# Chunked SSD attention and a GELU MLP on one core: the decay loads first, C scaled by GpSimd, a new order of the steps, and wide products in stage 1

## The chip, the cores and the metric

The kernel runs on one core of a Trainium2 chip. The time is device microseconds of one launch. A core has five engines that run side by side: TensorE (PE, with its weight loads PEld), VectorE (DVE), ScalarE (ACT), GpSimd (POOL) and SyncE (SP), which issues most of the DMAs.

## The reference

An attention over chunks (a state space model: 4 batches, 8 heads, 768 positions, head size 32, state size 16) gives 3072 rows of 256 columns, and a two-layer MLP with a tanh GELU follows.

```python
# per chunk of the sequence
cum = np.cumsum(log(clip(a)), axis=-1)
L = np.exp(cum[:, :, :, None] - cum[:, :, None, :]) * causal
M = einsum('bhin,bhjn->bhij', Cc, Bc) * L
y = einsum('bhij,bhjd->bhid', M, xc) + einsum('bhin,bhnd->bhid', Cc, state) * exp(cum)
state = exp(sum(la)) * state + sum over j of (B_j outer x_j) * exp(cum_last - cum_j)
# then, x = y as [3072, 256]
h = x @ w_in                       # 256 x 2048
out = gelu_tanh(h) @ w_out         # 2048 x 256
```

## The kernel before, in words

The sequence is cut into chunks of 128 positions, 6 for each of 4 batches, 24 in all. Two chunks make a pair `u` (0 to 11) of 256 tokens; pairs 0, 1 and 2 are batch 0.

The kernel is a list of named steps. A table, `ORDERED`, writes the order of all steps out by hand, and the engine that takes a step where there is a choice (`:A` ScalarE, `:D` VectorE, `:P` GpSimd, `:S` SyncE). Each engine runs its own instructions in that order. A word `~n` is a filler: matmuls of zeros, n times 128 columns, into the bank `yb`.

The front works for batch 0:

- `load_aq.0` to `load_aq.3` load the decays `a` of the first four chunks (four 16 KB loads into `aq_t`, on the queues of SyncE and ScalarE), `load_bc0.1` loads C and `load_bc0.0` loads B of these chunks (256 KB each into `bcf`), `load_x4` loads x, `load_a` the rest of the decays, `load_wi` and `load_wo` the four blocks each of w_in and w_out, 512 KB apiece.
- On VectorE, `clipq` (L328) clips the decays into `acq`, `Rq` (L331) scans them, `tpq` (L342) transposes, `recip0` (L348) takes the reciprocal `pt`. `mulb` (L416) scales B by the decays, `mulc.0` and `mulc.1` (L409) scale C by the reciprocals into `cz`, which `c_cz` has filled with zeros. `peq`, `c_sel` (the tiles `sel` and `selp`) and the small product `ppq` give `pendq`, the decay of each chunk.
- `tw.i` (L425) transposes the scaled C and B on TensorE, `ew.w.i` evicts the transposes (`ce`, `bh`). `x4` casts x.
- `XX.u` and `XD.u` (L563, L573) unpack x and form the state terms of pairs 0 and 1, `xn` evicts x. `c_bmask` builds a mask `bmask` on GpSimd, `c_par` reduces it.

Then, for every pair:

- `G.u` (L595) forms C times B into the banks `ga` and `gb`; `M.u.0` and `M.u.1` (L605) multiply by the causal mask `tri` on VectorE. For pair 0, half of that goes through ScalarE (`GE`, L610) and then `ME.2` and `ME.3` (L616 on GpSimd, L619 on VectorE).
- `S.u.k` (L676) carries the state on, `SP` (L683) prepares it for the next chunk.
- `Y.u` (L650, L659) sums both terms into `yb`, `yev.u` evicts it to `xm`.
- Stage 1, `s1.u.i` with i from 0 to 7 (L709): two blocks of 128 rows of h for the 256 tokens of the pair, four matmuls of 256 columns into one of two `hp` banks. `gelu.u.i` (L713) on ScalarE evicts to `gT`.
- Stage 2, `s2.u.k.q` (L727): four matmuls for a quarter of the 16 blocks, chunk k; `oev` evicts the sum, `store` writes it.

`clip`, `R` (L331), `pe` (L385, L387), `pp` (L393) and `pend` do for the rest of the decays what the `q` steps do for the first four chunks. `wi.q.k` and `wo.q.k` cast the weights to bfloat16.

Of the kernel before, what the change touches and what calls it, by code (L numbers as in the profile page):

```python
# [40 lines left out]
S.5.0 Y.4 gelu.3.6 G.5 load_x.6 load_x.8 yev.4.0.2:D s1.3.7 s2.3.0.0.o s1.4.0 gelu.3.7 s2.3.0.1.o
gelu.4.0 s1.4.1 s1.4.2 gelu.4.1 store_s.2.1 store_s.2.0 turn_s.2.1 F.2 store.1 M.5.1 store.4
load_s.2 turn_s.2.0 load_x.7 gelu.4.2 store.0 s2.3.0.2.o s2.3.0.3.o store.3 store.2 s1.4.3 gelu.4.3
s1.4.4 gelu.4.4 oev.6:D s2.3.1.0.o s1.4.5 s2.3.1.1.o s1.4.6 gelu.4.5 gelu.4.6 M.5.0 s1.4.7 gelu.4.7
SP.10 G.6 castx.6.None:P Y.5 D.6 S.6.0 castx.8.None:P S.6.1 M.6.0 s2.3.1.2.o s2.3.1.3.o SP.13 SP.12
yev.5.0.2:A s1.5.0 s1.5.1 oev.7:A gelu.5.0 s2.4.0.0.o s1.5.2 s2.4.0.1.o s2.4.0.2.o load_bc.3.0
mul.3.0 gelu.5.1 gelu.5.2 load_bc.3.1 mul.3.1 s1.5.3 s2.4.0.3.o gelu.5.3 oev.8:D s1.5.4 gelu.5.4
castx.7.None:P M.6.1 s1.5.5 gelu.5.5 s2.4.1.0.o s1.5.6 Y.6 gelu.5.6 D.7 G.7 S.7.0 s1.5.7 s2.4.1.1.o
s2.4.1.2.o s2.4.1.3.o gelu.5.7 load_x.9 castx.9.None:D S.7.1 yev.6.0.2:D s1.6.0 s1.6.1 gelu.6.0
oev.9:D store_s.3.1 gelu.6.1 s2.5.0.0.o s2.5.0.1.o s1.6.2 s1.6.3 s2.5.0.2.o gelu.6.2 SP.14  # L50
s2.5.0.3.o oev.10:A M.7.0 gelu.6.3 M.7.1 D.8 Y.7 yev.7.0.2:A G.8 store_s.3.0 s2.5.1.0.o s1.6.4
load_x.10 load_x.11 s2.5.1.1.o s2.5.1.2.o store.5 S.8.0 SP.16 gelu.6.4 s2.5.1.3.o castx.11.None:A
s1.6.5 s1.6.6 gelu.6.5 gelu.6.6 oev.11:D s2.6.0.0.o s1.6.7 gelu.6.7 s2.6.0.1.o s1.7.0 s1.7.1
gelu.7.0 store.6 s2.6.0.2.o gelu.7.1 s2.6.0.3.o oev.12:A turn_s.3.0 s1.7.2 gelu.7.2 s1.7.3 gelu.7.3
load_s.3 s2.6.1.0.o s2.6.1.1.o s1.7.4 s1.7.5 gelu.7.4 gelu.7.5 s2.6.1.2.o SP.15 s2.6.1.3.o store.9
s1.7.6 gelu.7.6 turn_s.3.1 M.8.1 M.8.0 F.3 D.9 Y.8 yev.8.0.2:A G.9 store.8 store.7 s1.7.7 S.9.0
S.9.1 oev.13:D gelu.7.7 s1.8.0 s2.7.0.0.o s1.8.1 s2.7.0.1.o s2.7.0.2.o s2.7.0.3.o gelu.8.0 SP.18
gelu.8.1 oev.14:D s1.8.2 s1.8.3 s2.7.1.0.o gelu.8.2 M.9.1 gelu.8.3 s2.7.1.1.o castx.10.None:A s1.8.4
gelu.8.4 s1.8.5 s2.7.1.2.o gelu.8.5 s2.7.1.3.o M.9.0 oev.15:D D.10 Y.9 S.10.0 S.10.1 G.10 M.10.1
s1.8.6 yev.9.0.2:A s1.8.7 gelu.8.6 SP.21 s2.8.0.0.o gelu.8.7 M.10.0 s1.9.0 s2.8.0.1.o gelu.9.0  # L60
s1.9.1 s1.9.2 SP.20 gelu.9.1 s2.8.0.2.o store.15 s1.9.3 s2.8.0.3.o gelu.9.2 store.11 gelu.9.3 s1.9.4
gelu.9.4 s1.9.5 gelu.9.5 SP.19 Y.10 D.11 S.11.0 G.11 yev.10.0.2:A s1.9.6 s1.9.7 store.10 gelu.9.6
oev.16:D s2.8.1.0.o M.11.1 s2.8.1.1.o s1.10.0 gelu.9.7 gelu.10.0 s1.10.1 s2.8.1.2.o gelu.10.1
s1.10.2 gelu.10.2 s2.8.1.3.o s1.10.3 gelu.10.3 s1.10.4 gelu.10.4 oev.17:D SP.22 s2.9.0.0.o
s2.9.0.1.o M.11.0 s1.10.5 Y.11 s2.9.0.2.o gelu.10.5 yev.11.0.2:A s1.10.6 s1.10.7 gelu.10.6
s2.9.0.3.o s1.11.0 gelu.10.7 s2.10.0.0.yb s1.11.1 gelu.11.0 s2.10.0.1.yb gelu.11.1 store.14 store.17
store.16 store.12 s1.11.2 gelu.11.2 oev.18:D s1.11.3 s2.10.0.2.yb s2.10.0.3.yb gelu.11.3 s2.9.1.0.o
s1.11.4 gelu.11.4 store.13 s1.11.5 gelu.11.5 s2.9.1.1.o s2.9.1.2.o s2.9.1.3.o oev.20:A oev.19:A
s1.11.6 s1.11.7 store.20 gelu.11.7 s2.10.1.0.o store.18 s2.10.1.1.o s2.10.1.2.o s2.10.1.3.o
s2.11.0.0.yb s2.11.0.1.yb s2.11.0.2.yb gelu.11.6 oev.21:A store.21 s2.11.0.3.yb s2.11.1.0.o  # L70
s2.11.1.1.o s2.11.1.2.o oev.22:A s2.11.1.3.o store.22 store.19 oev.23:A store.23
# [16 lines left out]
def kernel(  # L88
# [21 lines left out]
    T = 2 * Q  # L110
# [4 lines left out]
    NU = NCH // 2  # L115
# [12 lines left out]
    GT_BUFS = 5  # L128
# [56 lines left out]
    wi = moe_w_in.rearrange("(k d) f -> d k f", d=128)  # L185
# [531 lines left out]
    def f_s2(u, k, q, pool):  # L717
        gc = 2 * u + k
# [244 lines left out]
```

## Time and profile before

| | |
|---|---|
| time, median of 3 runs | 116.61 us (116.51 to 117.51) |
| the profiled execution | 117.7 us, its span 116.0 us |
| granted TensorE clock | 1.00 |
| busy in the span: TensorE, VectorE, ScalarE, GpSimd | 95%, 61%, 64%, 15% |
| chain that ended last | TensorE 88% of the span |

The profile is one execution. A row of the timeline or of the chain begins with its start and its length in microseconds from the start of the span, followed by engine, line and operation, `out<-in`, shapes and count. In brackets stands how long the engine had been idle before it, and on what. A row of a group gives busy time, mean ns of one, and the idle time before. Matmuls are pipelined, so the time from start to start is shorter than the length of one.

### The profile page before, as it was taken

To read this page: it belongs to the slowest core of one execution; us is meant where nothing else is said; L and a number is where in the kernel's file an instruction comes from. 1 tells how busy PE (TensorE), PEld (TensorE's weight loads), DVE (VectorE), ACT (ScalarE), POOL (GpSimd) and SP (SyncE) were. 2 spreads that over 40 slices of the span, in tenths; PEclk is the share of its full clock that TensorE was granted. 3 is DMA by queue.
4 is the path that set the end of the run, shared out by engine and by line. 5 is a ranking of instruction groups with operands and counts; after the bars stand their busy time and mean duration, and the time that the engine had idled before them with its cause. 6 is when DMAs were issued, how large, how long until landed. Compare 5 with 4: busy or idle time off the path is not lost.

```text
span 116.0 us, 3378 instructions
## 1 busy us (share of the span) xinstructions
PE 110.1 (95%) x1427; PEld 91.9 (79%) x1427; DVE 70.9 (61%) x139; ACT 73.7 (64%) x142; POOL 17.1 (15%) x35
## 2 busy tenths in 40 slices
PE   6969989999999999999999999999999999999990
PEld 2335568988788897998989889979979898999970
DVE  6589999789979995664967729221968326100000
ACT  3109679996469774766674567776767766776510
POOL 6552556622220220002000000000000000000000
DMA  3999997979979705999869893000014003200222
GB/s 71 235 242 249 403 325 197 359 138 210 221 122 206 156 4 165 178 199 255 164 174 177 206 90 104 0 0 6 0 51 139 0 6 107 74 0 6 90 96 85
DMA packets 43006, 15.97 MB, mean 138 GB/s; under 512 B 36656, under 2 KB 41456, under 8 KB 42992
## 3 DMA queue, kind: packets, MB, share of 16 engines
q1 hardware_dynamic: 42848, 15.68, 57.8%
q8 instruction: 11, 0.18, 0.6%
q10 hardware_dynamic: 144, 0.08, 0.3%
q14 instruction: 3, 0.02, 0.1%
HBM read 11.04 MB, written 3.93 MB: 129 GB/s over the span
## 4 chain that ended last, share of the span: by engine, by line
PE 88%; DVE 2%; ACT 2%; issue 0%
PE hp L709 37%; PE o_ps L727 34%; PE ga L595 3%; PE yb L727 3%; PE yb L659 3%; PE yb L650 3%; PE yb L697 2%; PE hp L628 1%; DVE cz L409 1%; PE hp L425 1%; ACT gT L713 1%; ACT xm L314 1%; DVE pe L387 1%; PE o_ps L563 0%; PE ga L484 0%; DVE s_new L676 0%
## 5 line engine op out<-in xcount | busy, mean ns | idle before, releaser
L713 ACT ACTIVATE gT<-hp 128x512 bf16<-128x512 f32 x96 | 53.9, 596 | 22.0 <-PE hp L709 21.4
L709 PE MATMUL hp<-xm,w_in_sb 128*128 128x256 bf16 x384 | 52.4, 273 | 0.7 <-ACT x L314 0.6
L727 PE MATMUL o_ps<-w_out_sb,gT 128*128 128x256 bf16 x352 | 47.5, 273 | 0.0
L709 PEld LDWEIGHTS <-w_in_sb 128*128 128x128 bf16 x384 | 41.4, 114 | 4.0 <-issue 3.2
L727 PEld LDWEIGHTS <-gT 128*128 128x128 bf16 x384 | 37.0, 98 | 4.2 <-issue 0.2
L605 DVE TENSOR_TENSOR m<-ga,tri 128x1024 bf16<-128x1024 f32 x12 | 14.6, 1216 | 0.3 <-PE gb L595 0.3
L318 DVE COPY o_sb<-o_ps 128x256 f32<-128x256 f32 x13 | 5.5, 423 | 14.6 <-PE o_ps L727 10.9
L605 DVE TENSOR_TENSOR m<-gb,tri 128x1024 bf16<-128x1024 f32 x11 | 13.4, 1214 | 0.0
L697 PE MATMUL yb<-wz 128*128 128x512 bf16 (+3 forms) x26 | 8.1, 459 | 1.1 <-DVE warm L222 1.1
L683 DVE SCALAR_TENSOR_TENSOR sp_new<-s_new,pend,bmask 128x256 bf16<-128x256 f32 x17 | 8.3, 503 | 0.1
L314 ACT ACTIVATE xm<-yb 128x512 bf16<-128x512 f32 x10 | 6.0, 598 | 2.7 <-PE yb L659 2.0
L316 POOL CAST x<-x_t 128x512 bf16<-128x512 f32 x6 | 3.7, 613 | 24.5 <-PE hp L709 9.9
L697 PEld LDWEIGHTS <-wz 128*128 128x128 bf16 x27 | 3.0, 121 | 5.0 <-issue 3.2
L314 ACT ACTIVATE o_sb<-o_ps 128x256 f32<-128x256 f32 x9 | 3.3, 384 | 4.5 <-PE o_ps L727 4.1
L659 PE MATMUL yb<-m,x 128*32 128x128 bf16 x192 | 6.2, 220 | 0.0
L676 DVE SCALAR_TENSOR_TENSOR s_new<-s_new,pend,hp 128x64 f32<-128x64 f32 x13 | 3.6, 279 | 4.1 <-PE hp L628 3.9
L650 PE MATMUL yb<-ce,sp_new 128*32 128x128 bf16 x160 | 5.3, 221 | 0.0
L674 DVE COPY s_new<-hp 128x64 f32<-128x64 f32 x3 | 0.7, 225 | 6.8 <-PE hp L628 6.8
L595 PE MATMUL ga<-ce,bh 32*128 32x256 bf16 x48 | 4.7, 272 | 0.0
L595 PE MATMUL gb<-ce,bh 32*128 32x256 bf16 x48 | 4.7, 273 | 0.0
L316 POOL CAST w_out_sb<-wf 128x512 bf16<-128x512 f32 x6 | 3.9, 672 | 3.7 <-DMA wf<-in_moe_w_out_dram 3.7
L659 PEld LDWEIGHTS <-x 128*32 128x32 bf16 x192 | 3.8, 97 | 0.7 <-issue 0.4
(109 smaller groups left out, 79.6 us busy)
## 6 DMA issues: line engine op xcount, KB each, us to landing
out_dram<-o_sb SPq DMA_DIRECT2D x24, 128.0 KB, 1.8
x_t<-in_x_dram SPq DMA_DIRECT2D x20, 128.0 KB, 3.8
wf<-in_moe_w_in_dram SPq DMA_DIRECT2D x4, 512.0 KB, 8.0
wf<-in_moe_w_out_dram SPq DMA_DIRECT2D x4, 512.0 KB, 8.6
bc_t<-in_B_dram SPq DMA_DIRECT2D x3, 384.0 KB, 4.3
bc_t<-in_C_dram SPq DMA_DIRECT2D x3, 384.0 KB, 4.3
scr<-bc SPq DMA_DIRECT2D x4, 192.0 KB, 2.0
x_t<-in_x_dram SPq DMA_DIRECT2D x1, 512.0 KB, 5.3
```

The lines of the kernel that those rows point to most:

```text
L314: nc.scalar.activation(o, i, AF.Copy)
L316: nc.gpsimd.tensor_copy(out=o, in_=i)
L318: nc.vector.tensor_copy(out=o, in_=i)
L595: nc.tensor.matmul(out=gbank(g)[:, 256 * k:256 * k + 256], lhsT=bh_of(2 * u + k)[gs], rhs=ce_of(2 * u + k)[gs], start=True, stop=True, til ...
L605: nc.vector.tensor_tensor(out=m_of(u)[:, 2 * i:2 * i + 2].rearrange("p g k e t -> p (g k e) t"), in0=gx[i].rearrange("p g (k t) -> p (g k) ...
L650: nc.tensor.matmul(out=y4[32 * j:32 * j + 32, k, w], lhsT=sp[:, 32 * h:32 * h + 32], rhs=ce_of(gc)[:, h % 2], start=first(j), stop=False, ...
L659: nc.tensor.matmul(out=y4[32 * j:32 * j + 32, k, w], lhsT=X16[u][:, k, 32 * h:32 * h + 32], rhs=m[:, h // 2, h % 2, :], start=first(j), st ...
L683: nc.vector.scalar_tensor_tensor(out=sp_new.rearrange("p (g d) -> p g d", g=4), in0=(XN[0][:, H * D:H * D + 64] if gc == 0 else state[("s" ...
L697: nc.tensor.matmul(out=t[:, 0:m * 128], lhsT=wz, rhs=w3.to_broadcast([128, m, 128]), start=True, stop=True, skip_group_check=True)
L709: nc.tensor.matmul(out=hp[:, j * T:(j + 1) * T], lhsT=w_in_k[:, w, q, k], rhs=xm[:, w, u * T:(u + 1) * T], start=(w == 0), stop=(w == 1))
L713: nc.scalar.activation(gts[u][:, 2 * i:2 * i + 2], hps.pop((u, i)).rearrange("p (j t) -> p j t", j=2), AF.Gelu_apprx_tanh)
L727: nc.tensor.matmul(out=ops[gc], lhsT=gts[u][:, fi, k * Q:(k + 1) * Q], rhs=w_out_sb[:, fi, :], start=(fi == 0 and (u > 0 or k == 0)), stop ...
```

## The change

Three things are changed. First, the four loads of the first decays go ahead of C and B on SyncE's queue, as they already do on ScalarE's, and GpSimd takes both halves of `mulc`, VectorE takes `mulb`. Second, the whole table `ORDERED` is new; the front's fillers and the places of the casts and evictions move with it. Third, for the pairs 6 to 11 stage 1 works on two pairs at once: 512 tokens of one block of 128 rows of h, two matmuls of 512 columns instead of four of 256. Pair 6's steps do the first eight blocks for pairs 6 and 7, pair 7's steps the other eight, and so on, so stage 2 of a pair waits for the GELUs of both.

```diff
+PAIR = 6
 ORDERED = """
-c_wz c_ident c_zero c_unp load_aq.2:A load_bc0.1 c_tri load_aq.1:S load_aq.3:S load_aq.0:A c_m8
...
+c_wz c_zero ~44 c_tri c_ident c_m4 load_aq.2:A c_m8 load_aq.1:S load_aq.0:A load_aq.3:S c_unp clipq
...
@@ f_s1
+        if u >= PAIR:
+            f, c = 8 * (u % 2) + i, u - u % 2
+            q, k = divmod(f, 4)
+            for w in range(2):
+                nc.tensor.matmul(out=hp, lhsT=w_in_k[:, w, q, k], rhs=xm[:, w, c * T:(c + 2) * T],
+                                 start=(w == 0), stop=(w == 1))
+            return
         for j in range(2):
@@ f_gelu
-        nc.scalar.activation(gts[u][:, 2 * i:2 * i + 2],
-                             hps.pop((u, i)).rearrange("p (j t) -> p j t", j=2),
+        nc.scalar.activation(gts[u][:, 2 * i:2 * i + 2].rearrange("p j t -> p (j t)"), hps.pop((u, i)),
                              AF.Gelu_apprx_tanh)
+
+    def g_of(u, k, f):
+        if u < PAIR:
+            return gts[u][:, f, k * Q:(k + 1) * Q]
+        t = gts[u - u % 2 + f // 8].rearrange("p (f j) t -> p f (j t)", j=2)
+        o = (u % 2) * T + k * Q
+        return t[:, f % 8, o:o + Q]
@@ f_s2
-            nc.tensor.matmul(out=ops[gc], lhsT=gts[u][:, fi, k * Q:(k + 1) * Q],
+            nc.tensor.matmul(out=ops[gc], lhsT=g_of(u, k, fi),
@@ the steps' dependencies
+            if u >= PAIR:
+                q = (8 * (u % 2) + i) // 4
-            s = s1[(u, i)] = add("E", f_s1, u, i, deps=[yev[u], win[(q, 0)], win[(q, 1)], s1.get((u, i - 1))])
+            s = s1[(u, i)] = add("E", f_s1, u, i, deps=[yev[u], yev[u + (u >= PAIR and u % 2 == 0)], win[(q, 0)], win[(q, 1)], s1.get((u, i - 1))])
+    for u in range(PAIR, NU):
+        for k, q in [(k, q) for k in range(2) for q in range(4)]:
+            s2[(2 * u + k, q)].deps += [gel[(u - u % 2 + q // 2, 4 * (q % 2) + i)] for i in range(4)]
+    s1[(NU - 1, 0)].deps.append(oev[2 * (NU - GT_BUFS) + 1])
```

What the new table moves is seen on the engines. VectorE, from the first decays to the scaled B and C, before (`m` is `c_m4`'s tile, `acq` the clipped decays, `rt` and `pt` the transposed decays and their reciprocals):

```order
L271 TENSOR_REDUCE sel_122<-ident 128x8
L273 COPY selp<-sel_122 128x128
L277 TENSOR_REDUCE m_121<-ident 128x4
L328 TENSOR_SCALAR acq<-aq_t 128x128
L331 SCALAR_TENSOR_TENSOR rq_t<-acq,ends 128x128
L342 STREAM_TRANSPOSE rt_125<-rq_t 128x128
L351 TENSOR_SCALAR peq<-m_121,acq,rq_t 128x4
L348 RECIPROCAL pt_127<-rt_125 128x32
L409 TENSOR_TENSOR cz<-bcf_100,pt_127 128x16x16 x2
L318 COPY bh_137<-o_ps 128x256
```

and in the changed kernel, from the clip on (its lines stand two lower in the file):

```order
L330 TENSOR_SCALAR acq<-aq_t 128x128
L333 SCALAR_TENSOR_TENSOR rq_t<-acq,ends 128x128
L344 STREAM_TRANSPOSE rt_125<-rq_t 128x128
L350 RECIPROCAL pt_127<-rt_125 128x32
L353 TENSOR_SCALAR peq<-m_121,acq,rq_t 128x4
L273 TENSOR_REDUCE sel_122<-ident 128x8
L275 COPY selp<-sel_122 128x128
L320 COPY pendq<-hp 128x4
L418 TENSOR_TENSOR bc0s_133<-bcf_100,rt_125 128x512
L320 COPY ce_135<-hp 128x256 x2
L268 TENSOR_REDUCE par<-bmask 128x1 x2
L320 CAST x4b<-x_t 128x512 x2
```

The reciprocal moves ahead of `peq`, `sel` and `selp` move behind the chain of the decays, both products with C leave VectorE, and the copy of `pendq`, the scaling of B, two evictions of C and both casts of x come to it.

GpSimd, from its zeroing of `cz` on, in the changed kernel:

```order
L256 MEMSET cz 128x1024
L411 TENSOR_TENSOR cz<-bcf_100,pt_127 128x16x16 x2
L238 MEMSET bmask 128x256
L240 AFFINE_SELECT bmask<-bmask 128x256
L242 AFFINE_SELECT bmask<-bmask 128x256
L618 AFFINE_SELECT m<-ge_140 128x512 x2
L318 CAST w_in_sb<-wf 128x512 x3
```

Before, `bmask` stood directly behind `cz`, then came the scaling of B, one cast of x, one select of `m` and four casts of `w_in_sb`. Now the scaling of C stands ahead of `bmask`, and both selects of `m` are GpSimd's.

TensorE, the first group of stage 1 for pair 6 in the changed kernel (`s1.6.0`, then stage 2 of an earlier pair):

```order
L712 LDWEIGHTS w_in_sb
L712 MATMUL hp<-xm,w_in_sb 128x512
L712 LDWEIGHTS w_in_sb
L712 MATMUL hp<-xm,w_in_sb 128x512
L742 LDWEIGHTS gT
```

Before, the group had four loads of weights and four matmuls of 256 columns at L709.

More of the change, by code (lines that the diff above doesn't have):

```diff
@@ L41 @@
[L41 to L58, printed above, removed]
@@ L71 @@
-s2.11.1.1.o s2.11.1.2.o oev.22:A s2.11.1.3.o store.22 store.19 oev.23:A store.23
+c_wz c_zero ~44 c_tri c_ident c_m4 load_aq.2:A c_m8 load_aq.1:S load_aq.0:A load_aq.3:S c_unp clipq
+Rq c_cz tpq recip0 peq c_sel ppq pendq:D c_warm load_bc0.1 mulc.0:P load_bc0.0 tw.1 mulb:D ew.0.1:D
+load_x4 load_a.0:A ew.1.1:D mulc.1:P tw.2 ew.0.2:A load_a.1:S tw.0 ew.0.0:A c_bmask ew.1.0:A c_par
+ew.1.2:A x4.0:D ~8 G.0 GE.3 GE.2 ME.3:P load_wi.0 ~8 x4.1:D XX.0 XD.0 xn.0:A ~8 xn.1:A ~4 ~8 M.0.0
+SP.0 S.0.0 XX.1 clip xn.2:A ME.2:P wi.0.1:P Y.0 yev.0.0.2:A wi.0.0:A S.0.1 XD.1 G.1 ~4 load_wi.1
```

80 lines of the change are left out of this document (48 added, 32 removed).

## The prediction

> **What bounds the kernel now.** I read the page's busy shares and its chain first, then the chain in order of time, then the stretches.
>
> ```profile
> PE 110.1 (95%) x1427; PEld 91.9 (79%) x1427; DVE 70.9 (61%) x139; ACT 73.7 (64%) x142; POOL 17.1 (15%) x35
> PE 88%; DVE 2%; ACT 2%; issue 0%
> 19.59:112.94 93.35, 93.34 (x1204) 82.66 (x1202) 54.33 (x94) 62.48 (x117) 6.44 (x10) 1.00 0.54 117
> ```
>
> The second line is the chain by engine, the third a stretch (length, then busy time of PE, PEld, DVE, ACT, POOL, then the granted clock 1.00). From 19.59 to 112.94 us TensorE stands still for 0.01 us in 93.35. There only fewer or quicker matmuls help, and every wait added is lost in full. Before that lies the front:
>
> ```profile
> 9.52 0.28 PE ga L595 x2
> 12.16 0.23 PE yb L659 x8
> 15.51 0.33 PE yb L393 x2
> 18.48 0.23 PE yb L650 x8
> 21.01 0.87 PE hp L709 x8
> 109.43 1.75 PE yb L727 x16
> 112.96 0.38 ACT o_sb L314
> ```
>
> These are pieces of the chain (start, length): the first G, the first Y at 12.16, the state decays at 15.51, the second Y at 18.48, then stage 1 of pair 1 at 21.01. The last matmul ends at about 112.9 and the tail after it is copy and store. So the end moves by what the front gains at about 21 us, by what the wide products save, and by what is lost in the dense part. The span of 116.0 us lies in an execution of 117.7 us; the median of the timed runs is 116.61. I work in the span and apply the difference to the median.
>
> **The wide products.** 192 matmuls of 256 columns (pairs 6 to 11) become 96 of 512.
>
> ```profile
> 7.20 0.65 PE L697 MATMUL yb<-wz 128*128 128x512 bf16 x3
> 7.63 0.22 PE L697 MATMUL yb<-wz 128*128 128x128 bf16 x1
> ```
>
> Two fills of 512 columns start at 7.20 and the narrow one behind them at 7.63: 0.215 us each. For 256 columns the chain above gives 1.75/16 = 0.1094 and 0.87/8 = 0.1088. Two narrow ones less one wide are 0.003 to 0.004 us, times 96 is 0.25 to 0.36. I take **0.25**, as stage 1's own row is the 0.1088; ends 0 and 0.4. The GELU keeps its 128x512 form, so ScalarE's work is the same.
>
> **Decay loads first.**
>
> ```profile
> 0.80 0.45 SPq L150 DMA_DIRECT2D bcf<-in_C_dram  x1
> 1.32 1.04 SPq L159 DMA_DIRECT2D aq_t<-in_a_dram  x2
> 2.40 0.43 SPq L150 DMA_DIRECT2D bcf<-in_B_dram  x1
> bcf<-in_C_dram SPq DMA_DIRECT2D x1, 256.0 KB, 3.1
> bcf<-in_B_dram SPq DMA_DIRECT2D x1, 256.0 KB, 4.2
> aq_t<-in_a_dram SPq DMA_DIRECT2D x2, 16.0 KB, 3.3
> 5.61 0.23 DVE L328 TENSOR_SCALAR acq<-aq_t 128x128 f32<-128x128 f32 x1 [1.33 <-DMA aq_t<-in_a_dram]
> 6.81 0.34 DVE L348 RECIPROCAL pt<-rt 128x32 f32<-128x32 f32 x1
> 2.32 1.34 DVE L261 COPY unp<-sub 128x32 bf16<-128x32 bf16 x1
> 2.41 0.94 POOL L254 MEMSET cz<- 128x1024 bf16 x1
> ```
>
> The first three rows are SyncE's issues, the next three the time from issue to landing, the rest VectorE and GpSimd. VectorE waits 1.33 us for the decays, whose last load was issued behind C. Issued at 0.80 and 1.32, the pair lands at 4.1 to 4.6 even with the old 3.3 us, sooner without C's 256 KB ahead. VectorE itself is free at about 3.7: the small copies stick behind GpSimd's zeroing of cz, which ends at 3.35. So the clip starts at **3.8** (ends 3.6 and 4.6; were it as late as now, that is a rival) instead of 5.61. From the clip to the end of the reciprocal are 1.54 us now and about 1.4 without `peq` between: 5.2. C is issued some 1.1 us later and lands at 1.9 + 3.1 = 5.0, in time; B stays at 2.4 + 4.2 = 6.6.
>
> **C scaled by GpSimd.**
>
> ```profile
> L409 DVE TENSOR_TENSOR cz<-bcf,pt x2: 414/658/903, 7.2 to 8.1; 128x256 bf16<-128x256 f32 x2
> 6.82 1.05 POOL L416 TENSOR_TENSOR bc0s<-bcf,rt 128x512 bf16<-128x512 f32 x1 [2.19 <-DVE rt L342]
> L435 DVE TENSOR_TENSOR bc0s<-bcf,rt 128x256 bf16<-128x256 f32 x1 | 0.4, 425 | 0.0
> L475 DVE TENSOR_TENSOR bc<-bc_t,pt 128x768 bf16<-128x768 f32 x3 | 2.8, 948 | 0.0
> 3.70 0.49 DVE L273 COPY selp<-sel 128x128 f32<-128x128 f32 x1
> 3.67 0.45 POOL L238 TENSOR_SCALAR_AFFINE_SELECT bmask<-bmask 128x256 bf16<-128x256 bf16 x1
> ```
>
> Two products of 256 elements on GpSimd are not in the trace. Its 512 took 1.05 us, so about 0.53 each (below: VectorE's 0.414; above: 1.05): 5.3 to 6.4. VectorE meanwhile runs `peq`, `sel` and `selp` (0.25, some 0.3, 0.49 by the rows), to 5.95; the small product `ppq` and its copy take until about 6.6. Then `mulb` waits for B at 6.6 and takes some 0.69 us, between 0.425 for 256 and 0.948 for 768 elements: all operands of the transposes at **7.3**. Now the second half of C ends at 8.1 + 0.4 = 8.5. That is 1.2 us, but it is not all kept.
>
> **Where it goes next.**
>
> ```profile
> 8.87 0.42 DVE L318 COPY bh<-o_ps 128x256 bf16<-128x256 bf16 x1 [0.38 <-PE o_ps L425]
> 9.96 1.22 DVE L605 TENSOR_TENSOR m<-ga,tri 128x1024 bf16<-128x1024 f32 x1
> 11.51 0.48 DVE L683 SCALAR_TENSOR_TENSOR sp_new<-o_ps,pendq,bmask 128x256 bf16<-128x256 f32 x1
> 12.04 1.32 DVE L331 TENSOR_TENSOR_SCAN r_t<-ac,ends 64x384 f32<-64x384 f32 x1
> 11.16 0.85 POOL L616 TENSOR_SCALAR_AFFINE_SELECT m<-ge 128x512 bf16<-128x512 bf16 x1 [2.20 <-ACT ge L610]
> 17.16 0.61 POOL L316 CAST w_out_sb<-wf 128x512 bf16<-128x512 f32 x1 [0.71 <-DMA wf<-in_moe_w_out_dram]
> 18.37 0.61 POOL L316 CAST w_in_sb<-wf 128x512 bf16<-128x512 f32 x1
> ```
>
> Between `mulb` and the first M, VectorE now has two evictions and two casts of x (0.42 each, 0.34 from start to start), and `par`, which waits for `bmask`, now built by GpSimd behind the two products (8.25): M at 9.05 instead of 9.96. Both masked halves ME are GpSimd's: 0.85 twice from about 9.4, done at 11.1. SP.0 (M plus 0.48) is done at 10.7. TensorE has XX.1 (0.5 us) ahead of Y.0 now, and XX.1 needs the bank that SP.0 and S.0 release: Y.0 at 11.4 instead of 12.16. ScalarE casts a half of the first w_in block (0.6) only behind Y.0's eviction, so stage 1 of pair 0 starts at about 13.15. On VectorE behind S.0 (10.85) come clip, S and SP (to 12.0, an SP held up some by GpSimd's cast), the scan (1.32, to 13.3), S and one M (to 14.7) and `pe`: the state decays at about 15.05 instead of 15.51. SP, a cast, S and the other M behind it are done at 17.45, so Y.1 at 17.5 instead of 18.48. But the fourth block of w_in stands in its queue behind the w_out block that GpSimd waited for until 17.16, and GpSimd cast it at 18.37; it lands between, and SyncE's queue has the same rows in the same places from B on. Its ScalarE half (0.6) stands between GELUs, so the last two groups of stage 1 for pair 0 cannot start before 18.9 to 19.1, and the one that needs the GELU behind the cast not before 19.4 to 19.7. With them stage 1 of pair 1 is at about 20.55 instead of 21.01. The front's term is **0.45** (ends: 0, and 0.9 if the block lands at 17.5). The fills before Y.0 are cover while TensorE waits and cost nothing as long as its clock is up.
>
> **In the dense part** I count nothing: same matmuls, same evictions. Tight places: pair 6 now needs Y.7 before its first group. Between G.7 and Y.7 TensorE has seven groups of four matmuls (half of 0.87 each), 3.05 us, and VectorE two M (1.22 each), SP (0.48) and S: about 3.2. Ends 0 to +0.4. The five fills behind the last product, about 1 us, run beside the last eviction and store.
>
> Sum: −0.45 − 0.25 = −0.7: span 115.3, that execution 117.0, median **115.9**.
>
> **Rivals.** *The port.* The two rows above show `cz` at 903 ns beside GpSimd's `mulb` and 414 ns without, and `selp` ended just after GpSimd's select: one engine waits out the other. If `selp` loses to both C products (6.5) and `mulb` then stands behind two selects of `bmask`, it ends at 8.35; the front gives 0, time 116.4. For it: those rows; against: GpSimd leaves gaps, and a VectorE operation that comes first holds GpSimd up instead. The Trainium skill, "SBUF — State Buffer", section "Who interferes with whom", says that a VectorE instruction with two SBUF inputs and a reading GpSimd instruction exclude each other for the whole instruction, and that issue order decides; the 903 ns agree.
>
> *The clock, slower.* TensorE's first fills are 44 units instead of 53.
>
> ```profile
> 1.88 1.06 PE L697 MATMUL yb<-wz 128*128 128x512 bf16 x2
> 2.31 1.06 PE L697 MATMUL yb<-wz 128*128 128x512 bf16 x2
> ```
>
> Early fills start 0.43 apart, double the 0.215 above; they end at about 5.5 now, and until 8.2 TensorE runs only small products and transposes, under 1 us of work. If it falls back to half pace there, some 2.7 us of fills, XX and Y up to 11.4 double, less the waits in it: Y.0 near 13.0, 0.9 later than now, less 0.25: 117.3. It decides if 2 us of near idleness is enough; stops of 0.7 us before 7.20 were not. The skill's "TensorE: Matmul & The Clock Gate", "Part 1: The HAM clock gate", puts the idle window at about 3.4 us; by it the clock would stay up here, and no run yet shows it.
>
> *The decays no sooner.* If the four loads land at 5.4 as now, C, `ppq` and `mulb` wait for them in the new order, all 1.8 later: Y.0 at 13.2, time 117.4. Against it: 16 KB loads with nothing ahead.
>
> *The weights land early.* Then 0.9 is kept: 115.4.
>
> **Chances.** Forecast 0.50 (115.9), port 0.20 (116.4), weights early 0.17 (115.4), clock 0.08, decays 0.05. A measurement of this kernel tells about 1% from no change, 1.17 us. Faster by more (below 115.44): half of the fourth case and the low edge of the first, 0.22; slower by more: the upper parts of the last two, 0.09; else 0.69. The range 115.2 to 117.0 holds the first three cases with the unknown prices and leaves the slow two out.
>
> **What would show it.** The clip near 3.8; `cz` on GpSimd at 5.3 to 6.4 in 0.5 us each; `mulb` ending by 7.4 rather than 8.3; the first M near 9.05; Y.0 near 11.4; stage 1 of pair 1 near 20.5; pairs 6 to 11 at 0.215 per product; no idle behind 21 us. A fill at 0.43 after 8 us, or the clip past 5, would make it wrong.

## The result: 0.7% slower, with a shorter profiled span

| | before | changed |
|---|---|---|
| time, median of 20 runs each, side by side | 117.02 us (116.33 to 117.83) | 117.73 us (117.01 to 118.58) |
| ratio, changed to before | | 1.0066 [1.0045, 1.0086] |
| the profiled execution, its span | 117.7 us, 116.0 us | 117.25 us, 115.3 us |

Here and below a median is over all runs of a kernel, while a ratio leaves out slow runs, over 1.5% above the kernel's fastest. Forecast were 115.9 us (115.2 to 117.0). The two profiled executions differ by the −0.7 us of span that the sum gave, and yet the kernel is 0.7 us slower. That the two traces agree with the sum is chance: the median span of the changed kernel's 20 runs is 115.8, so its trace is 0.5 us shorter than usual, and the trace of before is longer than usual, as shown below. The profile after is first read against the steps. The busy row and the chain by engine of the changed kernel, and one stretch of it from stage 1 of pair 1 to the last copy (length, busy time of PE, PEld, DVE, ACT, POOL, clock):

```profile
PE 110.7 (96%) x1326; PEld 81.8 (71%) x1333; DVE 71.9 (62%) x144; ACT 72.5 (63%) x139; POOL 15.5 (13%) x33
PE 79%; DMA 8%; SPq 5%; DVE 3%; issue 2%; POOL 1%; DVEq 0%
20.30:112.30 92.00, 91.53 (x1089) 71.16 (x1095) 54.45 (x92) 60.43 (x115) 5.08 (x8) 1.00 0.50 114
```

VectorE has 3% of the chain where it had 2%, and some of it now lies behind 20 us, as shown below. The 8% of DMA are one transfer of a w_out block, which ends at 16.02; GpSimd's cast follows, and then stage 1:

```profile
6.64 9.38 DMA wf<-in_moe_w_out_dram
16.72 0.60 PE L718 MATMUL hp<-xm,w_in_sb 128*128 128x256 bf16 x4 [0.25 <-POOL w_out_sb L318]
```

TensorE had stood still for only 0.25 us there, and a GELU that ended at 16.68 may as well have released it. So the chain's share says little of what this transfer costs. The front, from the timeline of the changed kernel, VectorE, GpSimd and TensorE:

```profile
3.44 0.23 DVE L330 TENSOR_SCALAR acq<-aq_t 128x128 f32<-128x128 f32 x1
5.37 0.23 DVE L275 COPY selp<-sel 128x128 f32<-128x128 f32 x1
6.54 0.75 DVE L418 TENSOR_TENSOR bc0s<-bcf,rt 128x512 bf16<-128x512 f32 x1 [0.31 <-DMA bcf<-in_B_dram]
9.05 1.22 DVE L607 TENSOR_TENSOR m<-ga,tri 128x1024 bf16<-128x1024 f32 x1
5.53 1.21 POOL L411 TENSOR_TENSOR cz<-bcf,pt 128x256 bf16<-128x256 f32 x2 [2.21 <-DMA bcf<-in_C_dram]
10.72 0.48 DVE L685 SCALAR_TENSOR_TENSOR sp_new<-o_ps,pendq,bmask 128x256 bf16<-128x256 f32 x1 [0.46 <-ACT x L316]
11.93 0.30 PE L661 MATMUL yb<-m,x 128*32 128x128 bf16 x8
14.88 0.40 PE L395 MATMUL yb<-pe,selp 64*128 64x24 f32 x2
20.30 0.87 PE hp L718 x8
```

Clip at 3.44 (forecast 3.8), C on GpSimd from 5.53 to 6.74 (5.3 to 6.4), B done at 7.29 (7.3), first M at 9.05 (9.05), state decays at 14.88 (15.05), stage 1 of pair 1 at 20.30 (20.55). Two signs are missed. There is idle time of TensorE behind 21 us, as shown below, and the first Y, Y.0, starts at 11.93 instead of 11.4. SP.0, which the forecast had done at 10.7, only starts at 10.72, behind a wait of 0.46 us for ScalarE's eviction of x. Otherwise the front of this trace was forecast well. What it was compared with was not.

### The profile page after: what moved, and what is told of

Read it like the earlier page. It is cut to its first block, busy times and chain, and to the rows that moved or that the text cites. A ratio compares the mean times of both kernels' runs of the same rounds, so it can differ in the third digit from the quotient of the medians.

```text
span 115.3 us, 3187 instructions
## 1 busy us (share of the span) xinstructions
PE 110.7 (96%) x1326; PEld 81.8 (71%) x1333; DVE 71.9 (62%) x144; ACT 72.5 (63%) x139; POOL 15.5 (13%) x33
## 4 chain that ended last, share of the span: by engine, by line
PE 79%; DMA 8%; SPq 5%; DVE 3%; issue 2%; POOL 1%; DVEq 0%
PE o_ps L742 32%; PE hp L712 18%; PE hp L718 16%; DMA wf<-in_moe_w_out_dram 8%; PE yb L742 3%; PE yb L652 3%; PE ga L597 2%; PE yb L661 2%; SPq L164 1%; SPq L192 1%; DVE m L607 1%; DVE rt L344 1%; PE hp L630 1%; PE yb L699 1%; SPq L152 1%
## 5 line engine op out<-in xcount | busy, mean ns | idle before, releaser
L742 PE MATMUL o_ps<-w_out_sb,gT 128*128 128x256 bf16 x352 | 48.6, 273 | 0.2
L718 PE MATMUL hp<-xm,w_in_sb 128*128 128x256 bf16 x192 | 26.7, 274 | 0.2 <-POOL w_out_sb L318 0.2
L712 PE MATMUL hp<-xm,w_in_sb 128*128 128x512 bf16 x89 | 25.2, 380 | 0.2
L718 PEld LDWEIGHTS <-w_in_sb 128*128 128x128 bf16 x192 | 20.1, 114 | 2.9 <-issue 1.9
L320 DVE COPY o_sb<-o_ps 128x256 f32<-128x256 f32 x10 | 4.2, 424 | 21.7 <-PE o_ps L742 21.7
L712 PEld LDWEIGHTS <-w_in_sb 128*128 128x128 bf16 x96 | 10.5, 114 | 4.3 <-issue 0.4
L699 PE MATMUL yb<-wz 128*128 128x512 bf16 (+1 forms) x28 | 9.4, 473 | 1.2 <-DVE warm L224 1.1
L316 ACT ACTIVATE o_sb<-o_ps 128x256 f32<-128x256 f32 x12 | 4.5, 382 | 3.6 <-PE o_ps L742 3.6
L316 ACT ACTIVATE xm<-yb 128x512 bf16<-128x512 f32 x8 | 4.8, 597 | 2.2 <-PE yb L661 1.6
L517 DVE TENSOR_SCALAR ce<-ch,par 128x768 bf16<-128x768 bf16 x6 | 2.2, 417 | 4.8 <-DMA ch<-scr 4.8
```

The lines of the kernel that those rows point to most:

```text
L316: nc.scalar.activation(o, i, AF.Copy)
L320: nc.vector.tensor_copy(out=o, in_=i)
L699: nc.tensor.matmul(out=t[:, 0:m * 128], lhsT=wz, rhs=w3.to_broadcast([128, m, 128]), start=True, stop=True, skip_group_check=True)
L712: nc.tensor.matmul(out=hp, lhsT=w_in_k[:, w, q, k], rhs=xm[:, w, c * T:(c + 2) * T], start=(w == 0), stop=(w == 1))
L718: nc.tensor.matmul(out=hp[:, j * T:(j + 1) * T], lhsT=w_in_k[:, w, q, k], rhs=xm[:, w, u * T:(u + 1) * T], start=(w == 0), stop=(w == 1))
L742: nc.tensor.matmul(out=ops[gc], lhsT=g_of(u, k, fi), rhs=w_out_sb[:, fi, :], start=(fi == 0 and (u > 0 or k == 0)), stop=(fi == NF - 1), s ...
```

## The experiments

Each ran beside the kernel before; the ratio is to it, with a 95% interval. The kernel before itself had median spans from 114.8 to 115.3 us in the different series of runs, so times and spans are compared within one series, or by their ratios. In the table at the end of this section stand marks from their profiles, and I point to it as the table of marks.

**The kernel before again, and its loads alone.** The first is the same kernel once more, the second moves only the decay loads.

> The kernel before, unchanged, for the spans of many executions and a second trace. The two traces at hand say that the change took 0.7 us out of the span (116.0 to 115.3), the timed runs that it added 0.7 us (117.02 to 117.73). If the trace of before was an execution slower than most (its 117.7 stands against a median of 117.02), the spans here have their median near 115.3 and the time around the span stays 1.7. If instead the span is near 116.0 in most executions, the time around it is about 1.0 and all of the loss lies outside the span.

116.55 us, ratio 1.0012 [0.9978, 1.0045], profiled at 116.79 us with a span of 115.0. The median of its spans is 114.8, with 1.73 us around the span, so the first case holds.

```diff
-c_wz c_ident c_zero c_unp load_aq.2:A load_bc0.1 c_tri load_aq.1:S load_aq.3:S load_aq.0:A c_m8
+c_wz c_ident c_zero c_unp load_aq.2:A load_aq.1:S c_tri load_aq.0:A load_aq.3:S load_bc0.1 c_m8
```

> The kernel before with one edit: all four decay loads are issued ahead of C and B. Theory: the decays land sooner, the clip starts at 3.7 instead of 5.6 and the front gains 0.5 to 1.0 us, 116.3. Rival: C lands a us later and the product with C starts no sooner, and the later weights hold stage 1: within 0.2 of 117.0.

116.55 us, 0.9972 [0.9945, 1.0000]. The loads alone are worth 0.3% or nothing: the first G starts at 8.76 instead of 9.37, but its chain then runs through a block of w_in.

```profile
6.74 11.23 DMA wf<-in_moe_w_in_dram
17.99 0.64 ACT w_in_sb L314
```

In the first of the two, the repeat, stage 1 of pair 1 starts at 20.26, not at 21.01 as in the trace that I had forecast from. Its first M, its first Y and its state decays:

```profile
9.80 1.22 DVE L605 TENSOR_TENSOR m<-ga,tri 128x1024 bf16<-128x1024 f32 x1 [0.26 <-PE gb L595]
11.94 0.30 PE L659 MATMUL yb<-m,x 128*32 128x128 bf16 x8
14.69 0.40 PE L393 MATMUL yb<-pe,selp 64*128 64x24 f32 x2
```

The old trace, with a span of 116.0, was an execution 0.7 to 1.2 us longer than usual: 0.7 against the runs beside which the change was timed (their median of 117.02 less 1.72 around the span, worked out, is 115.3), 1.2 against the repeat's 114.8. Why, is seen in five rows of VectorE's scan and GpSimd's cast of a weight block: first the cast of the old trace (its scan at 12.04 is shown above, 1.32 us), then a cast and a scan in run 1 of the chain below, then a scan and a cast in the run with one more instruction on GpSimd:

```profile
11.96 0.60 POOL L316 CAST w_in_sb<-wf 128x512 bf16<-128x512 f32 x1
12.25 0.61 POOL L318 CAST w_in_sb<-wf 128x512 bf16<-128x512 f32 x1 [1.49 <-DMA wf<-in_moe_w_in_dram]
12.31 1.36 DVE L333 TENSOR_TENSOR_SCAN r_t<-ac,ends 64x384 f32<-64x384 f32 x1
11.99 0.94 DVE L334 TENSOR_TENSOR_SCAN r_t<-ac,ends 64x384 f32<-64x384 f32 x1
12.03 1.32 POOL L319 CAST w_in_sb<-wf 128x512 bf16<-128x512 f32 x1 [1.59 <-DMA wf<-in_moe_w_in_dram]
```

Where the cast starts first, by 0.06 us in the second pair of rows, the scan takes 1.36 instead of 0.94; where the scan starts first, by 0.04, the cast takes 1.32 instead of 0.61. A wait for a weight block, which lands a little earlier or later, decides. The small product of `pe` meets the next cast in the same way; in the old trace this cast started at 13.61, 0.04 ahead. Old trace and repeat:

```profile
13.65 0.60 DVE L387 TENSOR_TENSOR pe<-pe,m 64x24 f32<-64x24 f32 x1
13.29 0.17 DVE L387 TENSOR_TENSOR pe<-pe,m 64x24 f32<-64x24 f32 x1
```

The old trace had lost both races, 0.38 and 0.43 us, on the way to its state decays at 15.44 in the timeline (15.51 in the chain of the prediction, where a piece begins when the one before it ends). The Trainium skill, "SBUF — State Buffer", section "Who interferes with whom", says that issue order decides which of the two blocks; these rows agree.

**Two parts taken back.** The changed kernel without the fillers behind the last product, and with narrow products throughout.

```diff
-oev.22:A store.21 ... oev.23:A store.23 ~4 ~7 ~4 ~4
+oev.22:A store.21 ... oev.23:A store.23
```

> The changed kernel without the five filler matmuls behind its last product. Theory fills: they hold the end of the program, outside the span, where the changed kernel has 1.95 us and the trace of before 1.7; the time falls by 0.2 to 0.3 us, 117.45 against 117.73. Rival: they end at 113.2, two us before the last store lands, and cost nothing: 117.7.

117.61 us, 1.0080 [1.0054, 1.0107]: the end fillers cost nothing.

```diff
-PAIR = 6
+PAIR = 12
```

> The changed kernel with stage 1 in products of 256 columns for all pairs, in the same order of steps. Theory as predicted: the wide products are worth 0.25 us, so this takes 0.25 more than the changed kernel, 118.0. Rival: the wide products or their weight loads bring a stall of their own, and narrow ones are as quick or quicker: 117.2 to 117.7.

117.72 us, 1.0093 [1.0060, 1.0126]. In the time that is 0 to 0.3 us. In the trace, from the fourth G to the last copy, 79.62 us with narrow and 79.21 with wide products (0.86 us for four of 512 columns below, 0.2150 each; 0.87 for eight of 256 above): 0.41, a little over the 0.25 of the sum.

```profile
62.30 0.86 PE hp L712 x4
```

In the repeat of the kernel before, also with narrow products, this stretch takes 79.30. So the new order by itself loses 0.3 us behind the fourth G between these two traces, and the wide products cover that.

**Half and half.** The new order up to the first product of stage 1 of pair 1, from there the old one with narrow products; and the other way round.

```diff
+ORDERED = changed table up to s1.1.0, then the steps left over in the order of before; PAIR = 12
```

> The changed order up to the first product of stage 1 of pair 1, and from there the order of before, with products of 256 columns throughout. Theory 1 (the loss lies in the new order behind pair 1): stage 1 of pair 1 starts at 20.3 as in the changed kernel, from there to the last copy 91.7 as in the kernel before, span 114.9, time 116.6; if the 0.25 us around the span also belongs to that part, 1.72 around it. Theory 2 (the loss lies in the front, and a typical execution of it is later than the profiled one): span 115.7, time 117.4 to 117.7.

117.20 us, 1.0021 [0.9994, 1.0047]; span, median of its runs, 115.2. The kernel before beside it had 115.3 (19 runs, 117.00 us).

```diff
+ORDERED = table of before up to s1.1.0, then the steps left over in the changed order; PAIR = 6
```

> The other half: the order of before up to the first product of stage 1 of pair 1, from there the changed order with products of 512 columns from pair 6 on. Theory 1: start at 20.3, 92.1 from there, span 115.4 to 115.8, time 117.3 to 117.7, with 1.95 around the span if that goes with this part. Theory 2: span 114.7, time 116.4.

117.80 us, 1.0081 [1.0046, 1.0117]; span 115.8. With the 115.3 of the kernel before in the same series, and 115.8 for the changed one (timed beside a kernel before of 117.02 us, the same level as this series' 117.00), these are the four corners: the new order behind pair 1, wide products included where it has them, costs 0.5 to 0.6 us of span with either front, and the new front gains 0 to 0.1. So theory 1 holds for the place of the loss; its figures for the first half (114.9, 116.6) were too low, since they set out from a lower level of the kernel before. Both halves have 2.0 us around the span, where the kernel before has 1.72, so that part of theory 1 falls.

**The chain behind the third G.** One place where the dense part loses is on the chain of the changed kernel. Behind the evictions of the first sequence's tail come two transposes of `rt`, the reciprocal ("issue" is its time here), the mask of pair 2 and the scaled B, and TensorE's transposes of B (`ga`) wait for them. The four matmuls ahead of these start at 26.53 and take 0.44, so TensorE stops for some 0.26 us:

```profile
22.37 0.29 DVE bn L320
22.67 0.39 DVE ce L456
23.09 0.52 DVE rt L344
23.62 0.54 DVE rt L344
24.22 0.94 issue
25.15 1.16 DVE m L607
26.31 0.87 DVE bc L477
27.23 0.51 PE ga L486 x6
```

In the repeat of the kernel before the same transposes follow directly on matmuls:

```profile
26.18 0.87 PE hp L709 x8
27.05 0.33 PE ga L484 x6
```

Five runs moved work there.

```diff
 # 1
-tp6.1 tp6.3 recip.1.4 s2.0.0.3.o s2.0.1.3.o M.2.0
+M.2.0 tp6.1 tp6.3 recip.1.4 s2.0.0.3.o s2.0.1.3.o
 # 2
-tp6.1 tp6.3 recip.1.4 ...  s2.1.0.2.o mul.1.1
+tp6.1 tp6.3 ...  s2.1.0.2.o recip.1.4 mul.1.1
 # 3
-wi.2.1:D ... wo.0.1:D ... wo.1.0:D
+wi.2.1:P ... wo.0.1:P ... wo.1.0:P
 # 4: as 3, and
-tp6.2 tp6.0 ... castx.2.None:P tp6.1 tp6.3
+tp6.2 tp6.0 tp6.1 tp6.3 ... castx.2.None:P
 # 5: the step of 4 without that of 3
```

> The changed kernel with one step moved: the first mask of pair 2 stands on VectorE ahead of the two transposes of rt and their reciprocal instead of behind them, as it did before. Theory (VectorE's chain from the second G of the dense part to its Y is where the new order loses): TensorE's stops of 0.1 to 0.3 us between 20.3 and 30 go, time 117.4. Rival (the chain is covered by stage 1 and stage 2 of pair 1): no change, 117.7.

> The changed kernel with one step moved on VectorE: the reciprocal of rt (0.97 us), which the scaled B of the second sequence does not need, stands ahead of the scaled C that does, behind the state product of the block, instead of ahead of the first mask of pair 2. Theory (VectorE's chain between the third G and the transposes of B sets TensorE's stops there, 0.27 us at 26.96 and 0.05 at 29.37 in the trace of the changed kernel): these stops go, the fourth G starts at 32.7 to 32.8 instead of 33.09, time 117.3 to 117.4. Rival (the stops are the end of something else): no change, 117.7.

> The changed kernel with three casts of weight blocks (the second half of the third w_in block, a half each of the first and second w_out block) on GpSimd instead of VectorE; the kernel before has none of these three on VectorE. Theory (VectorE is full from 14 to 32 us in the changed kernel, 19.2 us of 21, and these three casts of 0.7 to 0.8 us each make it so): G of pair 2 starts no later than now, the stop of 0.27 us at 26.96 goes, the fourth G starts at 32.5 to 32.7 instead of 33.09, time 117.1 to 117.4. Rival (GpSimd is then late with the weights, or the VectorE chain behind the third G is too long anyhow): 117.7 or later.

> The changed kernel with the three weight casts on GpSimd and, besides, the last two transposes of rt (0.53 us each) ahead of the evictions of the first sequence's tail instead of behind them. Theory (the loss between the third and the fourth G is a chain on VectorE that starts when these evictions are released by TensorE at 22.4, with work in it that could have run before, while VectorE stood idle 1.2 us between 20 and 23 in the run with the casts alone): the stops of 0.41 and 0.28 us go, from the third G to the fourth 9.6 to 9.9 instead of 10.34, span 115.3 to 115.5, time 117.0 to 117.2; with 63 instructions on GpSimd 1.72 around the span. Rival (the chain is as long behind the evictions, whatever stands ahead): 117.7.

> The changed kernel with the two transposes of rt moved ahead in the same way, the weight casts left on VectorE. Theory: VectorE has only 0.5 us idle there, so the evictions come 0.5 us later and the chain behind them is 1.06 shorter: stops of 0.3 us go, time 117.3 to 117.5, 1.97 around the span with 60 instructions on GpSimd. Rival: 117.7 or later.

Measured: 1: 118.30 us, 1.0100 [1.0053, 1.0147]. 2: 118.50 us, 1.0166 [1.0136, 1.0196]. 3: 117.70 us, 1.0082 [1.0044, 1.0120]. 4: 117.77 us, 1.0067 [1.0030, 1.0104]. 5: 118.09 us, 1.0108 [1.0072, 1.0144]. All five expectations of a gain failed in the time. In the traces, each stop of TensorE, in this order: of 1 and 3 at the transposes of B, of 2 at those of C, of 5 at the third G:

```profile
28.31 0.51 PE L486 MATMUL ga<-ident,bc 128*128 128x128 bf16 x6 [0.75 <-DVE bc L477]
27.74 0.51 PE L486 MATMUL ga<-ident,bc 128*128 128x128 bf16 x6 [0.24 <-DVE bc L477]
31.29 0.51 PE L486 MATMUL gb<-ident,bc 128*128 128x128 bf16 x6 [0.89 <-DVE bc L477]
23.53 0.28 PE L597 MATMUL ga<-ce,bh 32*128 32x256 bf16 x2 [0.61 <-DVE ce L456]
```

VectorE's chain there decides where TensorE stops. In run 1 the same work stands ahead of the scaled B, but the mask, now first, has to wait for the third G, and the transposes and the reciprocal wait behind it:

```profile
24.05 1.23 DVE L607 TENSOR_TENSOR m<-ga,tri 128x1024 bf16<-128x1024 f32 x1 [0.55 <-PE gb L597]
```

The stop at B becomes 0.75. In run 2 the reciprocal behind the scaled B makes the next stop 0.89; in run 5 the transposes ahead of the evictions hold up G by 0.61. Taking the casts off VectorE (3) does not shorten the chain, since VectorE then waits for TensorE ahead of it (0.84 us). In run 4 it had the room, and the stop at the transposes is gone:

```profile
27.94 0.44 PE hp L718 x4
28.38 0.34 PE ga L486 x6
```

From the third to the fourth G it took 9.67 us, 9.98 in the changed kernel and 10.34 in run 3, as expected. But its third G is at 24.36 (23.11 in the changed kernel): the scan and both products of `pe` lost their races (1.36, 0.57 and 0.55), and TensorE stood for 1.07 us ahead of the state decays:

```profile
16.01 0.40 PE L395 MATMUL yb<-pe,selp 64*128 64x24 f32 x2 [1.07 <-DVE pe L389]
```

Only one of the three casts met there, the one beside the second product of `pe`, is a cast that this run had moved; the other two stand on GpSimd in the changed kernel as well. In this trace, what was taken back behind 24 us was lost ahead of it. The median span of its ten runs is 116.1, against 115.0 for the kernel before beside it.

**C on VectorE.** The changed kernel with both halves of C on VectorE, and this once more with fillers in the gaps.

```diff
-mulc.0:P ... mulc.1:P
+mulc.0:D ... mulc.1:D
 # the second one also
-ppq pendq:D ... tw.1 mulb:D
+ppq ~16 pendq:D ... tw.1 ~16 mulb:D
```

> The changed kernel with both halves of C scaled by VectorE instead of GpSimd, in the same order. Forecast's reasoning (GpSimd takes 1.2 us of work off VectorE ahead of the scaled B): the scaled B ends at 7.7 instead of 7.29, first M at 9.4, stage 1 of pair 1 at 20.5 to 20.7, time 118.0. Rival (VectorE waited for B anyway until 6.5, and what bounds the front are weights and ScalarE): 117.7, no change.

121.78 us, 1.0370 [1.0323, 1.0417]: neither theory. The clock row of its page (tenths of the granted clock in 40 slices), TensorE's instructions at the place, and stretches in which the last number but two is the clock:

```profile
PEclk9965555999999999999999999999999999999999
5.87 0.39 PE L358 MATMUL hp<-peq,selp 128*128 128x4 f32 x2 [0.91 <-DVE selp L275]
6.86 0.40 PE L427 MATMUL hp<-ident,cz 128*128 128x128 bf16 x4 [0.60 <-DVE cz L411]
8.46 0.61 PE L427 MATMUL hp<-ident,cz 128*128 128x128 bf16 x4 [1.20 <-DVE cz L411]
5.50:7.00 1.50, 0.53 (x5) 0.44 (x6) 0.99 (x5) 0.00 (x0) 0.00 (x0) 1.00 1.18 288
7.00:8.00 1.00, 0.26 (x4) 0.08 (x2) 1.00 (x4) 0.00 (x0) 0.00 (x0) 0.63 0.91 251
14.00:20.00 6.00, 6.00 (x84) 2.79 (x83) 4.84 (x12) 2.13 (x5) 2.83 (x5) 0.50 0.97 288
20.00:22.00 2.00, 2.00 (x12) 1.15 (x11) 1.52 (x3) 1.33 (x3) 1.37 (x2) 0.77 1.02 365
```

The clock falls to half at 7.26 (0.63 over the slice from 7 to 8) and comes back at 20.9 (0.77 from 20 to 22), about 13.65 us later. In two of its six executions the mean clock was 0.94 (spans of 121.2 and 121.5), in three 0.97 (119.0 to 119.7). The sixth had 1.00 and yet a span of 120.4, which the clock does not explain. This is the rival "the clock, slower" of the forecast, one edit away from the changed kernel. There the transposes of C start at 6.21 behind a stop of 0.18:

```profile
6.21 0.40 PE L427 MATMUL hp<-ident,cz 128*128 128x128 bf16 x4 [0.18 <-POOL cz L411]
```

The Trainium skill, "TensorE: Matmul & The Clock Gate", section "Part 1: The HAM clock gate", has a free-running window of 3413 ns; the half pace lasted four of them. The Trainium skill's section "HAM oscillation — how this bites in real kernels", on the same page, asks for no gap above some 3.4 us; here no single stop was over 1.20 us, with 0.53 us of product time between 5.5 and 7.0, and the clock fell all the same. By this run a nearly idle window is enough.

> The changed kernel with C scaled by VectorE again, and 8 more warm-up products (0.215 us each at full clock) in two groups, behind the small product of the decays and behind the first transposes of C, where TensorE stood idle with C on VectorE. Theory (the 4 us that the run with C on VectorE lost are the clock, which fell to half at 7.26 us because TensorE had little to do between 5 and 8.5): the clock stays at 1.00, time 117.7 to 118.3, the rest of the difference being C's own lateness. Rival (the 4 us are VectorE's later work, and the clock only follows): 121.

119.24 us, 1.0217 [1.0186, 1.0249], clock 1.00 in every run, span 117.5. By the ratios, 1.0370, 1.0217 and 1.0066 for the changed kernel, the fillers take back some 1.8 us, and another 1.8 remain, more than the theory gave. The spans at the three levels of the clock, 117.5, 119.0 to 119.7 and 121.2 to 121.5, fit the theory; the execution of 120.4 at 1.00 does not. So it is likely, not shown, that the clock made about half of the loss. The rest is put down to C's own lateness; what the fillers themselves cost is not separated from it. In this order, moving C to VectorE costs 3.6 us in all.

**C on GpSimd in the old order.** With the decay loads first, all of C, or its first half, on GpSimd, B on VectorE.

```diff
-mulc.0:D mulc.1:D mulb:P
+mulc.0:P mulc.1:P mulb:D    # the second one: mulc.0:P mulc.1:D mulb:D
```

> The kernel before with the decay loads first, C scaled by GpSimd and B by VectorE, nothing else moved: the two named parts of the change in the old order. Theory (the weights bound the front, so what C gains is lost in the wait for w_in): time 116.4 to 116.6, as with the loads alone, although the first G starts at 8.2 or sooner instead of 8.76. Rival (the front's gain is kept to the end): 116.1. If GpSimd's masks are then late or the clock falls: 117 or more.

116.51 us, 0.9975 [0.9947, 1.0004], span (median) 114.65. As the theory has it: nothing more than the loads alone. The first G came at 8.51, later than the 8.2 given.

> The kernel before with the decay loads first, the first half of C on GpSimd, the second half and B on VectorE. GpSimd's program has 63 instructions again, as in the kernel before, instead of the 64 of the run with all of C on it. Theory (what lies around the span goes with the length of GpSimd's program: 1.72 at 63, 1.87 at 64): 1.72 around the span and a span of 114.6 to 114.8, time 116.3 to 116.5. Rival (the 1.87 came from GpSimd's work on C): 1.87, time 116.5 to 116.7.

116.69 us, 0.9987 [0.9953, 1.0021]; 1.72 around the span, as the theory had it, the span 114.7; the time is a little above the 116.5 given.

**The weights first.** The last block of w_in loaded and cast ahead of the first of w_out, in the old order with the decay loads first.

```diff
-load_wo.0 ... load_wi.3 ... wo.0.0:P ... wi.3.1:P ... s2.0.0.0.o s1.0.6 ... s2.0.1.0.o ... s1.1.0
+load_wi.3 load_wo.0 ... wi.3.1:P wo.0.0:P ... s1.0.6 ... s1.1.0 s2.0.0.0.o s2.0.1.0.o
```

> The kernel before with the decay loads first, and the last block of w_in loaded and cast ahead of the first block of w_out, the first two products of stage 2 moved behind the first of stage 1 of pair 1. Theory (what bounds the front in the end is the landing of the weights: in the run with the decay loads alone the chain is SyncE's issues up to 6.74 and then the transfer of w_in until 17.96): the last two products of stage 1 of pair 0 start 0.5 to 0.8 earlier, time 116.0 to 116.2, ahead of both kernels. Rival (the same bytes land at the same time, and w_out is then what is waited for): 116.5.

117.16 us, 1.0042 [1.0014, 1.0070]: no gain, and 0.7% behind the loads alone, so neither has it right. The last two products of stage 1 of pair 0 do start earlier, at 17.72 instead of 18.67, in part because a product of stage 2 now stands behind them. But the chain then runs through VectorE (two masks of pair 1, the transposes of `rt`, the scaled B) to TensorE at 19.03; w_out is not on it. No version beat both kernels by a difference that can be measured.

**Around the span.** One instruction that nothing uses, at the end of GpSimd's or VectorE's program.

```diff
+    nc.gpsimd.memset(pad, 0.0)    # the second one: nc.vector.memset
```

> The changed kernel with one more instruction, a zeroing of one column by GpSimd behind everything else, used by nothing. It asks where the 0.25 us around the span come from (1.72 in the kernel before and with C on VectorE, 1.95 to 2.0 in all others). Theory (the length or parity of GpSimd's or VectorE's program sets it): 1.72 around the span, time 117.5. Rival (it hangs on something else): 1.97, time 117.7.

117.39 us, 1.0060 [1.0026, 1.0093], but 2.11 us around the span instead of 1.97, so neither value was right: GpSimd's program moves it, not by parity. The time did not rise, since the median span is 115.3 here.

> The same with the extra instruction on VectorE instead of GpSimd. Theory (VectorE's program length): 1.72 around the span, time 117.5. Rival: 1.97, time 117.7.

117.72 us, 1.0113 [1.0073, 1.0153], 1.97 around it: VectorE's does not. Over all kernels, by the count of GpSimd's instructions in the built program (waits and register moves included), the mean time less span:

| GpSimd's instructions | kernels | us around the span |
|---|---|---|
| 57 | C on VectorE, without and with fillers | 1.74, 1.74 |
| 60 | changed, no end fillers, narrow, runs 1, 2 and 5 of the chain, one more on VectorE | 1.95 to 1.98 |
| 61 | one more on GpSimd | 2.11 |
| 62 | both halves | 2.00, 2.00 |
| 63 | before, again, loads alone, runs 3 and 4 of the chain, weights first, half of C | 1.71 to 1.73 |
| 64 | all of C, old order | 1.87 |

Equal counts have equal times within 0.03 us, whatever else differs, and the last run at 63 was foretold. Why a count gives its time stays open.

The profile of the run with one more on VectorE, which is the changed kernel otherwise, shows a third thing: a span of 116.9. Its chain has the round trip of the later sequences' B and C through memory on it, twice:

```profile
46.06 4.71 DMA bh<-scr
50.82 0.28 PE ga L598 x2
69.59 3.55 DMA ch<-scr
73.17 0.75 DVE ce L518 x2
```

Run 2 of the chain has the second of these on its chain too (3.19 us); none of the other 18 traces has either, the changed kernel's and the seven of the old order among them.

**The table of marks** (us): the scan, the state decays' product, and TensorE's lag, which is worked out: the start of the G less all matmul columns ahead of it in the program at 0.425 ns (0.1088 us for 256), products whose result has 32 rows as a quarter; at the last copy without the end fillers. Products that overlap make it fall along a kernel, so only differences between kernels count.

| profile | scan | decays | lag at third G | fourth G | end |
|---|---|---|---|---|---|
| before, as forecast from | 1.32 | 15.44 | 5.87 | 6.42 | 4.31 |
| before again | 0.94 | 14.69 | 5.13 | 5.51 | 3.40 |
| changed | 0.94 | 14.88 | 5.26 | 5.91 | 3.70 |
| changed, narrow | 0.94 | 15.09 | 5.46 | 5.95 | 4.15 |
| new front, old rest | 0.94 | 14.87 | 5.20 | 5.41 | 3.46 |
| old front, new rest | 0.94 | 14.79 | 5.51 | 6.30 | 4.06 |
| run 4 of the chain | 1.36 | 16.01 | 6.51 | 6.85 | 4.61 |
| one more on VectorE | 1.36 | 15.29 | 5.67 | 6.57 | 5.32 |

## Why the prediction was wrong

- **The baseline** failed first: "I work in the span and apply the difference to the median". The trace of before had lost two races that the repeat won. Against the repeat, the first Y at 11.93 stands beside 11.94 and the state decays at 14.88 beside 14.69: the front's term of 0.45 is 0, though most of its marks came as worked out. The first M is 0.75 earlier than in the repeat (9.05, 9.80), but by the first Y this is gone: SP.0 waits for ScalarE's eviction of x, a wait that the sum did not have. Behind that a mask of 1.21 us now stands on VectorE between the scan and `pe`; the sum had it, and only compared it with the scan of 1.32.
- **Two single traces** stood for two kernels. The trace of before lay 0.7 above its usual span (116.0, 115.3), the trace of the changed kernel 0.5 below (115.3, 115.8). Together they turn a loss of 0.5 into the gain of 0.7 that the sum gave. Besides, the median of three runs that the difference was applied to, 116.61, is 0.4 below that of 20 (117.02).
- **"In the dense part I count nothing"** was wrong by 0.5 to 0.6 us of span (the four corners). I had looked at pairs 6 and 7. In the traces the losses lie between the start of stage 1 of pair 1 and the fourth G, for the most part at a VectorE chain of 4.8 us (22.37 to 27.18) that the sum did not follow: +0.27 against the repeat from the third to the fourth G, and +0.66 of lag where the old front meets the new rest (0.38 at the third G, 0.41 to the fourth, −0.13 behind). Behind the fourth G the new order loses 0.3 more with narrow products, which the wide ones cover. That this chain makes TensorE stop is shown by the five runs that moved its work. That it makes the whole loss is not: none of them brought the time back. In two traces the round trips through memory are on the chain, and one of them loses 1 us more behind the fourth G than the changed kernel. How often that happens, 20 traces do not tell.
- **The time around the span** was taken as fixed, 1.7 us. It is 0.25 longer with GpSimd's 60 instructions than with 63. This is a third of the loss, and no step of the sum spoke of it.
- **The wide products** were about right: 0.41 in the traces, 0 to 0.3 in the times, for 0.25.
- **The rivals:** the port did not catch `selp` (0.23 us, done at 5.60), but in other executions of the new front it caught the scan (1.36 in runs 1, 3 and 4 of the chain). The clock was rightly named and is nearer than its 0.08: moving C alone brings it. The decays landed a little sooner than forecast (the clip at 3.44, not 3.8). The weights bound the old front with early loads (the chain of that run); in the new one the transfer of w_out is on the chain, with a stop of 0.25.

The loss adds up: 0.5 us of span (115.8 against 115.3, medians) and 0.25 around it, for the 0.7 that were measured side by side. From the repeat to the changed kernel the two traces show +0.3 of span (0.13 up to the third G, 0.27 to the fourth, −0.10 behind it). The remaining 0.2 fits the races and the round trips, which differ between executions; that is argued, not shown.

## What to carry to other kernels

Before a trace serves as the baseline, compare its own span with the median span of runs taken beside it, and look for instructions that take longer than their kind: a difference against an unlucky execution is not a gain. Do the same with the trace after the change, since a lucky execution hides a loss. When a hand-written order is replaced, follow each engine's chain through the stretch behind the edited one, not only its busy share, since a matmul engine that never waits can lose its cover by a few moved steps. An early front is only worth what the next slow chain leaves of it.

## What the runs showed of the hardware

- A race of 0.04 to 0.06 us between a cast on GpSimd and a scan on VectorE decides who loses 0.4 to 0.7 us (scan 0.94 or 1.36, cast 0.61 or 1.32).
- TensorE's clock fell to half for about 13.65 us although no stop was longer than 1.20 us.
- The time outside the span takes one value, within 0.03 us, for each length of GpSimd's program: from 1.71 to 1.73 us at 63 instructions to 2.11 at 61. Why is open.
